# Joining the half-array stays of inverse step 1 in a Fourier-mixing and SoLU kernel

## The chip, the cores and the metric

The kernel runs on one core of a Trainium2 chip. The engines are PE (TensorE, the matmul array), DVE (VectorE), ACT (ScalarE), POOL (GpSimd) and SP (SyncE, whose queue issues all DMAs here). The metric is device time in microseconds of one execution; lower is better. Most runs of one kernel agree within 0.3%.

## What is computed

The input x has 8 batches of 3136 rows and 256 columns, in float32. Each batch goes through a real Fourier transform along its rows, a complex 256 by 256 matrix with a bias, a soft threshold, and the inverse transform. The 25088 rows that result go through an expert layer with a SoLU in the middle.

```python
X = np.fft.rfft(x, axis=1)
Yr = Xr @ w_r - Xi @ w_i + b_r
Yi = Xr @ w_i + Xi @ w_r + b_i
Yr = np.sign(Yr) * np.maximum(np.abs(Yr) - lam, 0.0)
Yi = np.sign(Yi) * np.maximum(np.abs(Yi) - lam, 0.0)
y = np.fft.irfft(Yr + 1j * Yi, n=3136, axis=1)
...
h = y @ w_in
solu = h * softmax(h)
ln = (solu - mean(solu)) / np.sqrt(var(solu) + 1e-06) * g_ln
out = ln @ w_out
```

## The kernel before

**Factors of the transform.** 3136 is 98 times 32. Forward step 1 (`fwd1`, and `fwd1_plain` for batches 0 and 1) multiplies by a 98 by 98 matrix, forward step 2 (`fwd2`) does the 32 with its twiddle factors, and the inverse does the same backwards: inverse step 1 (`inv1`) and inverse step 2 (`inv2`). Between forward step 1 and step 2 a batch goes through DRAM (`s1`), and again between inverse steps 1 and 2 (`s2`). Most operands are split into a high and a low half in fp16, so that a product takes three fp16 matmuls; batch 0, and parts of batch 1, use plain float32 operands.

**Units.** The frequencies of a batch are handled in 13 units (`NU`). Units 0 to 11 have 128 rows of Y: two groups of 64, each with its own matrix. Unit 12 has only 64. For a unit, `fwd2` makes X in PSUM and splits it into `Xh` and `Xl`. `mix` multiplies by the weights (18 matmuls of 256 columns from batch 1 on, into two PSUM banks), adds the scaled bias `bias_y` with the first of two DVE operations that write `yt`, clips into `yc`, takes the difference `y` on POOL, casts it to `yh` on ACT and writes the rest `yl` on POOL.

**Inverse step 1.** For each unit, `inv1` runs for the pairs (yh, high matrix), (yl, high matrix) and (yh, low matrix), with real and imaginary parts each, one matmul for each group of 64 rows. The two matmuls of 64 rows stand on the two halves of the array and run side by side; a run of such matmuls is called a stay on half arrays here. Each of the two groups has its own PSUM bank, 256 columns for each unit. Batch 0 calls `inv1` for one unit at a time. Batches 1 to 7 call it for two units, so that two banks fill, and a stay has 24 matmuls. Behind it ACT copies each bank to the high part of `zout` and DVE writes the low part; then one DMA stores `zout` (512 KB from batch 1 on) to DRAM. The pool has two `zout` buffers.

**The expert layer.** A tile of 128 rows goes through `moe_head` (12 matmuls of 512 columns into two `ph` banks, a maximum `nm` on DVE for each, an Exp on ACT and a product on DVE for each half, into `u`), `moe_turn` (cast to `lh` and difference `ll`, each turned by a transposing DMA to `th` and `tl`) and `moe_tail` (24 matmuls of 256 columns into a `po` bank, one scaled copy, the store). A batch has 24.5 tiles; every second batch gets the shared tile.

**PSUM.** Eight banks are shared by kinds, each with a most: pf=5 (the transform from batch 1 on, inverse step 2 too), ph=5, po=2, and pb=8 for batch 0.

**Order of the work.** Nothing is issued as it is written. Each operation is noted with a key (`nc.key`), and `Plan.order` runs a list scheduler with a model of each engine's times: an engine takes, of the operations that can start within 50 ns of the first, the one with the lowest key. An operation can start when what it needs is done and its tiles have a free buffer and, in PSUM, a free bank. Matmuls in `nc.together()` are one operation for the plan, and `nc.reserve` makes it wait for its output's buffers as well. The order that comes out is fixed in each engine's queue; on the chip, semaphores keep it right.

**Keys of a batch.** `first` is the key of the first head of batch b, L its 24 or 25 tiles. In that time lie `front_b(b + 1)`, that is `fwd2`, `mix` and `inv1` of the next batch, and `front_a(b + 2)`, that is the peaks, the scales and `fwd1` of the one after. In `front_b`, step n does `fwd2` of unit n, `mix` of unit n − 1, and `inv1` of the units up to n − lag.

**Lines that the change touches.** `fa_s` (line 485) is the plain matrix of forward step 1, loaded first of all and used by `fwd1_plain` only (line 633). `Xs` (line 686) is the float32 sum of X's parts, from batch 1 on, with one buffer. `bias_y` is made in `set_scales` (lines 566 and 567) with two buffers, and read at lines 731 and 754. `yh` and `yl` (lines 774 and 775) have four buffers each. `inv1` is lines 780 to 824, `front_b` lines 1144 to 1157, and its keys are at line 1185.

Of the kernel before, what the change touches and what calls it, by code (L numbers as in the profile page):

```python
# [12 lines left out]
F32 = mybir.dt.float32  # L13
F32R = mybir.dt.float32r
BF16 = mybir.dt.bfloat16
F16 = mybir.dt.float16
U32 = mybir.dt.uint32
AF = mybir.ActivationFunctionType
ALU = mybir.AluOpType
# [5 lines left out]
S, N1, N2 = 3136, 98, 32  # L25
H = N1 // 2
Q = (H - 1) // 2
# [5 lines left out]
S_SCALE, B_SCALE, Z_SCALE, X_SCALE = 2.0**-7, 2.0**-5, 2.0**-11, 2.0**-11  # L33

LOW = 2.0**11
# [416 lines left out]
def fft_mix_solu_kernel(ctx: ExitStack, tc, x, w_r, w_i, b_r, b_i, w_in, w_out, g_ln, fa, fbf, fsf, iaf, fa16, fb, fs, gb, gs, ia, out):  # L452
    nc = Plan(tc.nc)
    B, _, D = x.shape
    FF = w_in.shape[1]
    P = 128
    ND = D // P
# [10 lines left out]
    fp = Pool(ctx.enter_context(tc.tile_pool(name="fp", bufs=2)), 2)  # L468
# [4 lines left out]
    def front_psum(b):  # L473

        return banks.tile("pf" if b else "pb")
# [3 lines left out]
    def load(shape, src, name, pool=const, dtype=F32, **kw):  # L479
        t = pool.tile(shape, dtype, name=name, **kw)  # L480
        nc.sync.dma_start(t, src)
        return t

    nc.key = -300
    fa_s = load([N1, N1], fa, "fa_s")
    nc.key = 0
    ident = const.tile([P, P], F32, name="ident")
    ones = const.tile([P, P], F32, name="ones")
# [40 lines left out]
    peaks, scales = {}, {}  # L529
# [13 lines left out]
    def set_scales(b):  # L543

        top = sp.tile([P, 1], F32, name="top", bufs=2)
        pk = peaks.pop(b)
        m = pk.shape[0]
        nc.vector.tensor_reduce(top[:m], pk, AX.X, ALU.max)
        pw = front_psum(b)
        nc.tensor.transpose(pw[:1, :m], top[:m], ident[:m, :m])  # L550
        v = sp.tile([1, 2], F32, name="v", bufs=2)
        nc.vector.tensor_reduce(v[:, :1], pw[:1, :m], AX.X, ALU.max)
        nc.vector.tensor_scalar(v[:, 1:], v[:, :1], gain[:1], bias_top[:1], ALU.mult, ALU.add)
        nc.vector.tensor_scalar(v, v, 2.0**-100, None, ALU.max)
        nc.vector.tensor_scalar(v.bitcast(U32), v.bitcast(U32), 0x7F800000, None, ALU.bitwise_and)
        pw = front_psum(b)
        nc.tensor.matmul(pw[:, :2], ones[:1], v, start=True, stop=True)
        un = sp.tile([P, 4], F32, name="un", bufs=4)
        sc = sp.tile([P, 5], F32, name="sc", bufs=4)
        nc.vector.tensor_scalar(un[:, :2], pw[:, :2], 2.0**-14, None, ALU.mult)  # L560
        nc.vector.tensor_scalar(sc[:, :2].bitcast(U32), un[:, :2].bitcast(U32), -1.0, float(254 << 23), ALU.mult, ALU.add)
        nc.vector.tensor_scalar(sc[:, 4:], sc[:, :1], S_SCALE * B_SCALE, None, ALU.mult)
        nc.vector.tensor_scalar(un[:, 3:], un[:, :1], 1.0 / S_SCALE, sc[:, 1:2], ALU.mult, ALU.mult)
        nc.vector.tensor_scalar(sc[:, 2:3], sc[:, 1:2], LAM, None, ALU.mult)
        nc.vector.tensor_scalar(sc[:, 3:4], sc[:, 1:2], -LAM, None, ALU.mult)
        bias_y = fp.tile([P, 2, D], F32, name="bias_y", bufs=2)
        nc.vector.tensor_scalar(bias_y, bias_t, sc[:, 1:2], None, ALU.mult)
        nc.vector.tensor_scalar(un[:, 2:3], un[:, 3:], w_un, None, ALU.mult)
        scales[b] = dict(
            x=sc[:, 0:1], X=sc[:, 4:], lam=(sc[:, 2:3], sc[:, 3:4]), mix=un[:, 2:3], bias=bias_y, y=un[:, 1:2]  # L570
        )
        if b:
            set_h_scale(b)

# [31 lines left out]
    PLAIN, PLAIN_Z = 2, 1  # L606
# [32 lines left out]
    QG = 4  # L639
    raw, bins = {}, {}  # L640
    s2 = {}
    zouts = {}
    Xs, Ys = {}, {}
# [18 lines left out]
    NU = Q // 2 + 1  # L662
# [96 lines left out]
    def mix(b, u):  # L759
        n, _ = unit_size(u)  # L760
        half = 2 * N2
        M = n * half
        t = mix_split(b, u) if b else mix_first(u)
        c = fp.tile([P, 2, D], F32, name="yc", bufs=2)
        up, down = scales[b]["lam"]
        y = fp.tile([P, 2, D], F32, name="y", bufs=2)
        if b == 0:

            nc.scalar.activation(c[:M], t[:M], AF.Relu, bias=down[:M], scale=-1.0)
            nc.scalar.activation(t[:M], t[:M], AF.Relu, bias=down[:M], scale=1.0)  # L770
        else:
            nc.vector.tensor_scalar(c[:M], t[:M], up[:M], down[:M], ALU.min, ALU.max)
        nc.gpsimd.tensor_sub(y[:M], t[:M], c[:M])
        yh = fp.tile([P, 2, D], F16, name="yh", bufs=4)
        yl = fp.tile([P, 2, D], F16, name="yl", bufs=4)
        nc.scalar.copy(yh[:M], y[:M])
        nc.gpsimd.tensor_sub(yl[:M], y[:M], yh[:M])
        Ys[b, u] = yh, yl

    def inv1(b, u0, u1):  # L780


        n, _ = unit_size(u0)
        half = 2 * N2
        K = half * n
        g, gi = divmod(2 * u0, QG)
        part, dtype = ((2, D), F16) if b >= PLAIN_Z else ((D,), F32)
        if n == 1:
            zo, gi = fp.tile([K, 1, *part], dtype, name="zs", bufs=1), 0
        else:  # L790
            if gi == 0:
                zouts[b] = fp.tile([P, QG, *part], dtype, name="zout")
            zo = zouts[b]
        w = u1 - u0
        pz = [front_psum(b) for _ in range(n)]
        nc.reserve(zo[:, gi : gi + n * w])
        with nc.together():
            for u in range(u0, u1):
                yh, yl = Ys.pop((b, u))
                for k, (t, j) in enumerate(((yh, 0), (yl, 0), (yh, 1))):  # L800
                    for ri in range(2):
                        for i in range(n):
                            rows = slice(i * half, (i + 1) * half)
                            gw = gs_s[:, ri, j] if n == 1 else gb_s[g][rows, u % 2, ri, j]
                            nc.tensor.matmul(
                                pz[i][:K, (u - u0) * D : (u - u0 + 1) * D], gw, t[rows, ri], start=k + ri == 0, stop=k + ri == 3
                            )
        m = n * w
        for i in range(n):
            pv = pz[i][:K, : w * D].rearrange("p (u e) -> p u e", u=w)  # L810
            if b < PLAIN_Z:
                zv = zo[:, gi : gi + m].rearrange("p (u i) e -> p u i e", i=n)[:, :, i]
                nc.scalar.activation(zv, pv, AF.Copy, scale=Z_SCALE)
                continue
            zv = zo[:, gi : gi + m].rearrange("p (u i) t e -> p u i t e", i=n)[:, :, i]
            nc.scalar.activation(zv[:, :, 0], pv, AF.Copy, scale=Z_SCALE)
            nc.vector.scalar_tensor_tensor(zv[:, :, 1], zv[:, :, 0], -LOW, pv, ALU.mult, ALU.add)
        if b >= PLAIN_Z:
            zo = zo.rearrange("p q t e -> p q (t e)")
        if n == 1:  # L820
            nc.sync.dma_start(s2[b][4 * Q :].rearrange("c (n m) -> (c n) m", n=N2), zo[:, 0])
        else:
            v = s2[b][: 4 * Q].rearrange("(q c) m -> q (c m)", c=4).rearrange("q (r m) -> r q m", r=P)
            nc.sync.dma_start(v[:, g * QG + gi : g * QG + gi + m], zo[:, gi : gi + m])

# [206 lines left out]
    bias_t = const.tile([P, 2, D], F32, name="bias_t")  # L1034
# [6 lines left out]
    gs_s = load([2 * N2, 2, 2, 2 * N2], gs, "gs_s", dtype=F16)  # L1041
# [5 lines left out]
    fb_s, gb_s = {}, {}  # L1047
# [95 lines left out]

    def front_b(b, key, step):

        lag = 4 if b == 0 else 3
        for n in range(NU + lag):
            nc.key = key + n * step
            for fn, u in ((fwd2, n), (mix, n - 1)):
                if 0 <= u < NU:  # L1150
                    fn(b, u)
            u = n - lag
            if u == NU - 1 or 0 <= u < NU and b == 0:

                inv1(b, u, u + 1)
            elif 0 < u < NU and u % 2:
                inv1(b, u - 1, u + 1)

    nc.key = -140
    set_scales(0)  # L1160
# [16 lines left out]
    first = 0  # L1177
    for b in range(B):
        L = 24 + b % 2
        if b == 0:  # L1180
            front_a(1, -40, 0.5)
        if b + 2 < B:
            front_a(b + 2, first + 6, (L - 6) / 17)
        if b + 1 < B:
            front_b(b + 1, first + (6 if b == 0 else -2), (L - (8 if b == 0 else 4)) / (NU + 3))
        groups = 0
        for n in range(L):
            while groups < N2 // G2 and groups * G2 * N96 <= n * P:
                nc.key = first + n - 3
                inv2(b, groups)  # L1190
                groups += 1
            nc.key = first + n
            heads.append(moe_head((b, n if n < 24 else None)))
            nc.key = first + n + 0.5
            turned.append(moe_turn(*heads.pop(0)))
            nc.key = first + n + 1
            moe_tail(*turned.pop(0))
        first += L
# [25 lines left out]
```

## Time and profile before

| | us |
|---|---|
| median of 3 runs | 1615.39 |
| lowest and highest | 1613.5 and 1616.07 |
| profiled execution | 1616.65 |
| its span, first to last instruction | 1614.9 |
| PE busy in it | 1577.4 |
| DVE busy | 1326.1 |
| ACT busy | 1238.8 |
| POOL busy | 1123.6 |

The profile is of one execution. Every instruction is recorded under the line of a helper (L342), so its groups are told apart by the tiles that they write and read: `pf<-yh,gb` is a matmul of inverse step 1 that reads yh and the matrix gb. Durations of matmuls overlap, because the array is a pipeline: what one of them costs is read from the starts of the neighbours. In a row of a stretch of time stand its length, the busy time of PE, PE's weight loads, DVE, ACT and POOL, each with a count of instructions, then the granted clock of PE, the share of the DMA engines and GB/s. A row of such a stretch for one tile alone has only the engines that work on it. In a row of a tile stand the least, median and greatest duration in ns and the first and last start in us.

### The profile page before, as it was taken

The numbers are of one execution on the slowest core, as the hardware profiler recorded it, in microseconds if no ns is written. First come the engines' busy times: TensorE is split into PE (matmuls) and PEld (weight loads), VectorE is DVE, ScalarE is ACT, GpSimd is POOL, SyncE is SP. The second block draws the span as 40 slices with busy tenths as digits, with TensorE's granted clock in tenths as the row PEclk, the third lists the DMA queues.
The fourth block names the chain that finished last, engine by engine and source line by source line (L and its number), as shares of the span: only waits on it lengthen the run. The fifth ranks groups of instructions, "written<-read, shape, count | busy, mean of one in ns | idle before, by whom it ended". The sixth has DMA issues, their size and how long they took to land.

```text
span 1614.9 us, 38042 instructions
## 1 busy us (share of the span) xinstructions
PE 1577.4 (98%) x13040; PEld 1126.1 (70%) x13040; DVE 1326.1 (82%) x3423; ACT 1238.8 (77%) x2576; POOL 1123.6 (70%) x1889
## 2 busy tenths in 40 slices
PE   5979999999999999999999999999999999999998
PEld 3545877678766777667776687666876677776675
DVE  4779789996799877898789978899688888877775
ACT  4667678886789867898679876798678877778886
POOL 0555776677866777667777687766976677777676
PEclk8989999999999999999999999999999999999999
DMA  8868955996579965899669984699857986677676
GB/s 236 277 228 206 210 145 133 227 240 155 127 185 232 226 151 121 185 243 217 135 130 224 279 169 118 135 246 258 166 112 165 204 172 129 122 146 154 140 129 115
DMA packets 533923, 290.25 MB, mean 180 GB/s; under 512 B 427642, under 2 KB 503964, under 8 KB 533728
## 3 DMA queue, kind: packets, MB, share of 16 engines
q1 hardware_dynamic: 533728, 287.82, 78.5%
q8 instruction: 102, 1.67, 0.4%
q14 instruction: 93, 0.76, 0.2%
HBM read 107.89 MB, written 77.07 MB: 115 GB/s over the span
## 4 chain that ended last, share of the span: by engine, by line
PE 92%; DVE 3%; ACT 2%; DMA 1%; issue 1%; POOL 0%; SPq 0%; DVEq 0%; ACTq 0%; POOLq 0%
PE po L342 31%; PE ph L342 30%; PE pf L342 27%; PE pb L342 4%; DVE u L342 1%; DVE xl L342 1%; DVE nm L342 1%; DMA zt<-s2f 0%; ACT u L342 0%; DMA s2f<-zs 0%; ACT junk L342 0%; DMA bin<-s1f 0%; DMA s1f<-tl 0%; DVE av L342 0%; DMA th<-lh 0%
## 5 line engine op out<-in xcount | busy, mean ns | idle before, releaser
L342 POOL TENSOR_TENSOR ll<-u,lh 128x1024 f16<-128x1024 f32 x196 | 424.4, 2166 | 98.5 <-ACT lh L342 95.4
L342 PE MATMUL po<-wout,th 128*128 128x256 f16 x3136 | 374.5, 273 | 4.1 <-DMA th<-lh 1.9
L342 PEld LDWEIGHTS <-th 128*128 128x128 f16 x3136 | 305.4, 98 | 64.9 <-issue 4.4
L342 ACT ACTIVATE u<-ph,m,hsb 128x512 f32<-128x512 f32 x384 | 295.9, 776 | 52.3 <-DVE m L342 51.7
L342 DVE TENSOR_REDUCE nm<-ph 128x1 f32<-128x512 f32 x392 | 264.5, 685 | 79.7 <-PE ph L342 78.6
L342 DVE SCALAR_TENSOR_TENSOR u<-ph,ch,u 128x512 f32<-128x512 f32 x392 | 281.5, 747 | 23.1 <-ACT u L342 13.7
L342 PE MATMUL ph<-win_hi,ring_hi 128*128 128x512 f16 x768 | 291.9, 380 | 0.2 <-DVE u L342 0.2
L342 PE MATMUL ph<-win_lo,ring_hi 128*128 128x512 f16 x768 | 291.5, 380 | 0.0
L342 PE MATMUL ph<-win_low,ring_lo 128*128 128x512 f16 x768 | 291.3, 379 | 0.0
L342 ACT CAST lh<-u 128x1024 f16<-128x1024 f32 x196 | 205.7, 1049 | 53.1 <-DVE u L342 52.8
L342 PEld LDWEIGHTS <-ring_hi 128*128 128x128 f16 x1536 | 146.8, 98 | 140.5 <-issue 6.5
L342 ACT ACTIVATE junk<-u,total 128x1024 bf16<-128x1024 f32 x196 | 226.1, 1154 | 7.1 <-POOL total L342 6.6
L342 PE MATMUL po<-wout,tl 128*128 128x256 f16 x1568 | 203.4, 273 | 0.8 <-DMA tl<-ll 0.8
L342 PEld LDWEIGHTS <-tl 128*128 128x128 f16 x1568 | 150.7, 98 | 35.0 <-issue 3.4
L342 POOL TENSOR_TENSOR y<-yt,yc 128x512 f32<-128x512 f32 (+1 forms) x104 | 133.1, 1281 | 59.4 <-ACT yt L342 32.7
L342 POOL TENSOR_TENSOR yl<-y,yh 128x512 f16<-128x512 f32 (+1 forms) x104 | 122.3, 1178 | 40.3 <-ACT yh L342 39.3
L342 PE MATMUL pf<-w_hi,Xh 128*128 128x256 f16 (+1 forms) x546 | 149.1, 273 | 0.0
L342 PE MATMUL pf<-w_hi,Xl 128*128 128x256 f16 (+1 forms) x546 | 148.9, 273 | 0.0
L342 PE MATMUL pf<-w_lo,Xh 128*128 128x256 f16 (+1 forms) x546 | 148.8, 273 | 0.0
L342 ACT ACTIVATE o<-po,r 128x256 f32<-128x256 f32 x196 | 93.2, 475 | 59.6 <-PE po L342 30.7
L342 PEld LDWEIGHTS <-ring_lo 128*128 128x128 f16 x768 | 75.1, 98 | 91.1 <-DVE last_lo L342 0.3
L342 PEld LDWEIGHTS <-Xh 128*128 128x128 f16 (+1 forms) x1196 | 113.9, 99 | 24.8 <-issue 1.9
(196 smaller groups left out, 2922.5 us busy)
## 6 DMA issues: line engine op xcount, KB each, us to landing
xt<-in_x_dram SPq DMA_DIRECT2D x108, 392.0 KB
zt<-s SPq DMA_DIRECT2D x56, 392.0 KB
s<-zout SPq DMA_DIRECT2D x42, 512.0 KB
s<-av SPq DMA_DIRECT2D x48, 392.0 KB
bin<-s SPq DMA_DIRECT2D x36, 512.0 KB
out_dram<-o SPq DMA_DIRECT2D x128, 96.0 KB
out_dram<-o SPq DMA_DIRECT2D x136, 64.0 KB
bin<-s1f SPq DMA_DIRECT2D x12, 512.0 KB
```

The source lines that it names most:

```text
L342: getattr(engine, name)(*args, **kw)
```

## The change

Inverse step 1 takes four units at a time in batches 1 to 7: for units 0 to 3, 4 to 7 and 8 to 11 the 48 matmuls stand in one group, over four PSUM banks, and both `zout` buffers are reserved ahead of it. The evictions and the two stores follow. Batch 0 and unit 12 go as before. For the two more buffers (a fifth `yh` and a fifth `yl`), `bias_y` goes from two buffers to one and is now made in `mix` of a batch's unit 0, and the plain matrix `fa_s` is no tile of its own but lies in the first use of `Xs`. The lag of `inv1` in `front_b` goes from 3 to 2 from batch 1 on, the start of the front's keys from `first` − 2 to `first` − 3 (from batch 2 on), and their step from (L − 4) / 16 to (L − 5) / 16.

```diff
-    fa_s = load([N1, N1], fa, "fa_s")
+
+    fa_s = fp.tile([P, ND, 2, 2 * N2], F32, name="Xs", bufs=1).rearrange("p h i c -> p (h i c)")[:N1, :N1]
+    nc.sync.dma_start(fa_s, fa)
...
-        bias_y = fp.tile([P, 2, D], F32, name="bias_y", bufs=2)
-        nc.vector.tensor_scalar(bias_y, bias_t, sc[:, 1:2], None, ALU.mult)
...
+        if u == 0:
+            scales[b]["bias"] = fp.tile([P, 2, D], F32, name="bias_y", bufs=1)
+            nc.vector.tensor_scalar(scales[b]["bias"], bias_t, scales[b]["up"], None, ALU.mult)
         t = mix_split(b, u) if b else mix_first(u)
...
-        yh = fp.tile([P, 2, D], F16, name="yh", bufs=4)
-        yl = fp.tile([P, 2, D], F16, name="yl", bufs=4)
+        yh = fp.tile([P, 2, D], F16, name="yh", bufs=5)
+        yl = fp.tile([P, 2, D], F16, name="yl", bufs=5)
...
-        pz = [front_psum(b) for _ in range(n)]
-        nc.reserve(zo[:, gi : gi + n * w])
+        work = []
+        for u2 in range(u0, u1, 2):
...
+            us = range(u2, min(u2 + 2, u1))
+            work.append((g, gi, zo, us, [front_psum(b) for _ in range(n)]))
+        nc.reserve(*(zo[:, gi : gi + n * len(us)] for _, gi, zo, us, _ in work))
         with nc.together():
-            for u in range(u0, u1):
...
+            for g, _, _, us, pz in work:
+                for u in us:
+                    yh, yl = Ys.pop((b, u))
+                    for k, (t, j) in enumerate(((yh, 0), (yl, 0), (yh, 1))):
+                        for ri in range(2):
+                            for i in range(n):
+                                rows = slice(i * half, (i + 1) * half)
+                                gw = gs_s[:, ri, j] if n == 1 else gb_s[g][rows, u % 2, ri, j]
+                                at = slice((u - us[0]) * D, (u - us[0] + 1) * D)
+                                nc.tensor.matmul(pz[i][:K, at], gw, t[rows, ri], start=k + ri == 0, stop=k + ri == 3)
+        for g, gi, zo, us, pz in work:
...
-        lag = 4 if b == 0 else 3
+        lag = 4 if b == 0 else 2
...
-            elif 0 < u < NU and u % 2:
-                inv1(b, u - 1, u + 1)
+            elif 0 < u < NU and u % 4 == 3:
+                inv1(b, u - 3, u + 1)
...
-            front_b(b + 1, first + (6 if b == 0 else -2), (L - (8 if b == 0 else 4)) / (NU + 3))
+            front_b(b + 1, first + (6 if b == 0 else -3), (L - (8 if b == 0 else 5)) / (NU + 3))
```

More of the change, by code (lines that the diff above doesn't have):

```diff
@@ L565, in set_scales @@
         nc.vector.tensor_scalar(sc[:, 3:4], sc[:, 1:2], -LAM, None, ALU.mult)
-        bias_y = fp.tile([P, 2, D], F32, name="bias_y", bufs=2)
-        nc.vector.tensor_scalar(bias_y, bias_t, sc[:, 1:2], None, ALU.mult)
         nc.vector.tensor_scalar(un[:, 2:3], un[:, 3:], w_un, None, ALU.mult)
-        scales[b] = dict(
-            x=sc[:, 0:1], X=sc[:, 4:], lam=(sc[:, 2:3], sc[:, 3:4]), mix=un[:, 2:3], bias=bias_y, y=un[:, 1:2]
-        )
+        scales[b] = dict(x=sc[:, 0:1], X=sc[:, 4:], lam=(sc[:, 2:3], sc[:, 3:4]), mix=un[:, 2:3], y=un[:, 1:2], up=sc[:, 1:2])
         if b:
@@ L785, in inv1 @@
         K = half * n
-        g, gi = divmod(2 * u0, QG)
         part, dtype = ((2, D), F16) if b >= PLAIN_Z else ((D,), F32)
[L788 to L794, printed above, removed]
-        pz = [front_psum(b) for _ in range(n)]
-        nc.reserve(zo[:, gi : gi + n * w])
-        with nc.together():
-            for u in range(u0, u1):
[L799 to L824, printed above, removed]
+        work = []
+        for u2 in range(u0, u1, 2):
+            g, gi = divmod(2 * u2, QG)
+            if n == 1:
+                zo, gi = fp.tile([K, 1, *part], dtype, name="zs", bufs=1), 0
+            else:
+                if gi == 0:
+                    zouts[b] = fp.tile([P, QG, *part], dtype, name="zout")
+                zo = zouts[b]
+            us = range(u2, min(u2 + 2, u1))
+            work.append((g, gi, zo, us, [front_psum(b) for _ in range(n)]))
@@ new lines, in inv1 @@
+        for g, gi, zo, us, pz in work:
+            w = len(us)
+            m = n * w
+            for i in range(n):
+                pv = pz[i][:K, : w * D].rearrange("p (u e) -> p u e", u=w)
+                if b < PLAIN_Z:
+                    zv = zo[:, gi : gi + m].rearrange("p (u i) e -> p u i e", i=n)[:, :, i]
+                    nc.scalar.activation(zv, pv, AF.Copy, scale=Z_SCALE)
+                    continue
+                zv = zo[:, gi : gi + m].rearrange("p (u i) t e -> p u i t e", i=n)[:, :, i]
+                nc.scalar.activation(zv[:, :, 0], pv, AF.Copy, scale=Z_SCALE)
+                nc.vector.scalar_tensor_tensor(zv[:, :, 1], zv[:, :, 0], -LOW, pv, ALU.mult, ALU.add)
+            if b >= PLAIN_Z:
+                zo = zo.rearrange("p q t e -> p q (t e)")
+            if n == 1:
+                nc.sync.dma_start(s2[b][4 * Q :].rearrange("c (n m) -> (c n) m", n=N2), zo[:, 0])
+            else:
+                v = s2[b][: 4 * Q].rearrange("(q c) m -> q (c m)", c=4).rearrange("q (r m) -> r q m", r=P)
+                nc.sync.dma_start(v[:, g * QG + gi : g * QG + gi + m], zo[:, gi : gi + m])
```

## The prediction

> **What bounds the kernel now.** I read the page's head first, then busy time by stretches, then PE's waits, then single stretches of PE in order of time.
>
> ```profile
> span 1614.9 us, 38042 instructions
> ...
> PE 1577.4 (98%) x13040; PEld 1126.1 (70%) x13040; DVE 1326.1 (82%) x3423; ACT 1238.8 (77%) x2576; POOL 1123.6 (70%) x1889
> ```
>
> ```profile
> 0.00:40.00 40.00, 22.53 (x75) 13.39 (x76) 16.55 (x37) 17.06 (x35) 3.46 (x10) 0.81 0.81 235
> ...
> 80.00:120.00 40.00, 31.05 (x182) 17.61 (x180) 30.45 (x61) 26.43 (x56) 22.41 (x17) 0.88 0.70 230
> ...
> 1000.00:1200.00 200.00, 199.33 (x1739) 144.81 (x1738) 173.21 (x451) 159.12 (x337) 146.11 (x246) 1.00 0.81 184
> ...
> 1600.00:1615.00 15.00, 8.08 (x69) 6.16 (x67) 2.81 (x10) 5.93 (x12) 6.43 (x12) 1.00 0.52 105
> ```
>
> ```profile
> PE pb L342 <- DMA bin<-s1f: 15.0, 1, 15.0
> PE pf L342 <- DMA zt<-s2f: 8.9, 1, 8.9
> PE po L342 <- DMA th<-lh: 1.9, 2, 1.6
> PE pf L342 <- DVE u L342: 1.5, 1, 1.5
> ```
>
> PE (third column of a stretch) is idle 1614.9 − 1577.4 = 37.5 us. Of these 17.5 lie in the first 40 us, 9.0 in 80 to 120, 6.9 in the last 15: 33.4 in all, 4.1 for the rest. The two long waits are loads at the start, which the change doesn't touch. Behind the start the kernel lasts as long as PE has work, at full clock (1.00), so a microsecond taken off PE's stream comes off the span, if the other engines still keep it fed. How near they are to not doing so shows within one batch:
>
> ```profile
> 345.00:465.00 120.00, 120.00 (x1149) 92.68 (x1148) 94.67 (x246) 88.75 (x188) 93.93 (x148) 1.00 0.68 146
> 465.00:513.00 48.00, 46.54 (x310) 29.84 (x308) 45.91 (x105) 41.82 (x81) 31.56 (x57) 1.00 0.98 230
> 513.00:541.00 28.00, 28.00 (x224) 17.92 (x222) 27.44 (x82) 23.29 (x55) 16.53 (x36) 1.00 1.11 269
> ```
>
> The first row is the stretch with forward step 2, mix and inverse step 1 (the front's second half): PE full, DVE (fifth column) 79%. The second is forward step 1, the third the peaks: DVE 96% and 98%. The 1.46 us that PE lost there is the 1.5 us wait above. So PE sets the end, DVE is close behind in 76 of some 195 us of a batch.
>
> **The change part by part.** *Stays on half arrays.* A stay is a run of matmuls of 64 rows, two side by side. Its price, from PE in order of time:
>
> ```profile
> 1000.05 1.04 PE L342 MATMUL po<-wout,tl 128*128 128x256 f16 x8
> 1000.93 0.38 PE L342 MATMUL ph<-win_hi,ring_hi 128*128 128x512 f16 x1
> ...
> 1016.70 1.04 PE L342 MATMUL po<-wout,tl 128*128 128x256 f16 x8
> 1017.66 0.39 PE L342 MATMUL pf<-yh,gb 64*128 64x256 f16 x4
> 1017.89 0.38 PE L342 MATMUL pf<-yl,gb 64*128 64x256 f16 x4
> 1018.11 0.60 PE L342 MATMUL pf<-yh,gb 64*128 64x256 f16 x8
> 1018.55 0.38 PE L342 MATMUL pf<-yl,gb 64*128 64x256 f16 x4
> 1018.77 0.38 PE L342 MATMUL pf<-yh,gb 64*128 64x256 f16 x4
> 1019.08 0.39 PE L342 MATMUL ph<-win_hi,ring_hi 128*128 128x512 f16 x1
> 1019.31 0.38 PE L342 MATMUL ph<-win_lo,ring_hi 128*128 128x512 f16 x1
> 1019.52 0.38 PE L342 MATMUL ph<-win_low,ring_lo 128*128 128x512 f16 x1
> ```
>
> Read starts, since the durations overlap. Going in: eight po matmuls take 1000.93 − 1000.05 = 0.88 us before a full-array neighbour, but 1017.66 − 1016.70 = 0.96 before the stay: 0.08. Coming out: the last four half matmuls last 1019.08 − 1018.77 = 0.31, where four in the middle take 0.22 (1017.89 to 1018.11): 0.09. The first full matmul afterwards takes 0.23 where the next takes 0.21: 0.01 to 0.02. A stay of two units lasts 1.42 (1017.66 to 1019.08); one more unit inside costs 0.66 (the yl group of unit one to that of unit two, 1017.89 to 1018.55). So four units in one stay take 1.42 + 2 × 0.66 = 2.74 against 2 × 1.42 = 2.84, and the way in and the slow first matmul are paid once instead of twice: 0.10 + 0.09 + 0.01 = 0.20 us less for each pair of stays joined.
>
> ```profile
> L342 PE MATMUL pf<-yh,gb x672: 269/269/280, 198.4 to 1416.7; 64*128 64x256 f16 x168
> ```
>
> A two-unit stay has 16 yh matmuls, so 672 are 42 stays, six for each of seven batches; they become 21. Batch 0 and each batch's odd last unit keep theirs. Sum: 21 × 0.20 = **4.2 us less**, all on PE's stream. The changed bank inside a stay has no row; a changed bank without a changed array (po to ph at 1000.93) costs nothing, so I take nothing, and at worst the 0.10 would be lost on each: 2.1 us.
>
> The Trainium skill, "TensorEngine Tiling (Array Packing)", Key Properties, says that a changed tiling mode drains the array; the trace agrees, with 0.08 going in and 0.09 coming out. By the warm constant of "TensorE: Matmul & The Clock Gate", Single matmul latency (398 cycles at 2.4 GHz, 166 ns), an estimate would be two undrained latencies, 0.33 us a stay, 7.0 us in all and 1608.4 us; the measured 0.20 decides.
>
> *Evictions.* Their number stays; they now come four at a time.
>
> ```profile
> L342 ACT ACTIVATE zout<-pf x84: 573/594/625, 199.9 to 1418.6; 128x512 f16<-128x512 f32 x84
> L342 DVE SCALAR_TENSOR_TENSOR zout<-zout,pf x84: 668/680/690, 200.5 to 1419.5; 128x512 f16<-128x512 f16 x84
> L342 SPq DMA_DIRECT2D s<-zout x42: 365/457/1777, 201.8 to 1422.8; - x42
> ```
>
> Four take 4 × 0.68 = 2.7 us of DVE behind the stay instead of 1.4; what queues behind them are the heads' reductions, and PE waits for those only when it has no other bank. Taken as nothing, because the front's stretch leaves DVE 21% free; its price when that cover is gone is the slow rival's. The two stores of one stay leave SP back to back, so a tail's transpose can stand 0.46 us longer: nothing to 21 × 0.46 = 9.7 us. I take nothing, by the nearest row: PE waited for th twice in the whole run. Both zout buffers must be empty ahead of a stay; the last stores are then about 58 us old (1218 us over 21 stays), and 1.05 MB at the 184 GB/s of the stretch 1000 to 1200 takes 5.7.
>
> *Y's buffers.* A stay holds four of five yh and yl, so the second unit behind it can't cast yh on ACT until the stay's first unit is read, 0.66 us into the stay; behind that cast on ACT stand Exps and evictions, and PE waits for their banks. The plan puts the cast behind the stay by its own clock. Nothing, with 0.66 × 21 = 14 us at the far end.
>
> *Scaled bias and plain matrix.*
>
> ```profile
> L342 DVE TENSOR_SCALAR bias_y<-bias_t,sc x8: 475/479/481, 25.2 to 1225.7; 128x512 f32<-128x512 f32 x8
> ...
> L342 PE MATMUL pf<-xt,fa_s x32: 590/592/672, 94.9 to 134.9; 98*98 98x512 f32 x32
> ...
> L342 ACT ACTIVATE Xs<-pf,sc x13: 367/474/519, 152.4 to 271.6; 128x256 f32<-128x256 f32 x12, 128x128 f32<-128x128 f32 x1
> ```
>
> The bias is the same DVE operation, moved from the scales to ahead of the batch's first yt: at worst 7 × 0.48 = 3.4 us late, at best 0.48 off the chain of the first scales. It needs the scales only, which are long done, and PE has heads while it runs: nothing. The plain matrix lies in Xs; Xs's first writer now waits for the last plain matmul, over by 135.6, and it started at 152.4 anyway: nothing. Its load stays SP's first.
>
> *Keys.* The front gets a start one key lower and a shorter step; step 1's last stay comes at key 13.6 of a batch of 24 instead of 16.8. This moves work between the three stretches but takes none away. I price it in the rivals.
>
> Sum: −4.2 us. The profiled execution took 1616.65 us, 1.3 above the median of the runs, so 1612.4 in its terms and 1615.4 − 4.2 = **1611.2 us** in the median's.
>
> **The rivals.** A difference under about 0.2% (3.2 us) can't be told from none here.
>
> *Slower: banks.* A stay of four starts only when four of pf's five banks are free at one moment. The mix just before it holds two until both yt operations are through:
>
> ```profile
> L342 DVE SCALAR_TENSOR_TENSOR yt<-pf,un,bias_y x91: 724/743/753, 165.6 to 1409.5; 128x512 f32<-128x512 f32 x84, 64x512 f32<-64x512 f32 x7
> L342 DVE SCALAR_TENSOR_TENSOR yt<-pf,un,yt x91: 731/744/753, 167.3 to 1412.2; 128x512 f32<-128x512 f32 x84, 64x512 f32<-64x512 f32 x7
> ```
>
> The place is the start of each batch's front, where hardly a head is there to fill in (reductions nm on DVE, a head has two):
>
> ```profile
> 541.00:587.00 46.00, 2.55 (x7) 1.00 0.89 191
> 587.00:660.00 73.00, 15.77 (x30) 1.00 0.56 124
> ```
>
> If PE stands for both yt there, once a batch, it is 7 × 1.49 = 10.4 us: 1615.4 − 4.2 + 10.4 = 1621.6. At 0.20 us a stay the gain is gone, at (4.2 + 3.2) / 21 = 0.35 it is slower by what can be told. Against it: PE stayed full in 345 to 465 and has tails and inverse step 2 there, which take other banks or one of pf. For it: a batch's front comes denser. The Trainium skill, "TensorEngine Tiling (Array Packing)", PSUM Bottleneck, warns of just this: tiling speeds TensorE, not the emptying of PSUM; in the trace so far no wait of PE names such a bank, so the rule has not bitten with two units a stay.
>
> *No change that can be told.* The gain is there, but the new order, which the planner works out afresh everywhere, brings stalls like the 1.5 us above: one of 0.4 us a batch is 7 × 0.4 = 2.8, and 1614.0 us. Here belongs too that the joined stay saves half (2.1 us, 1613.3).
>
> *Faster than forecast.* The front done earlier leaves more heads for the two stretches where DVE is full, which are PE-rich. Then the mid-run idle of 4.1 us goes as well: 1607.1.
>
> **How the numbers follow.** Forecast (1608.5 to 1612.1) 0.43, faster than that 0.13, no change 0.28, slower 0.16. Together: faster 0.56, same 0.28, slower 0.16. The range is 1606.0 to 1621.5: below lies little of the faster case (0.05), above the slow rival with stalls at more than one stay a batch (0.08). The forecast's own range is 1608.5 to 1612.1.
>
> **What would show it.** The after trace should have 21 stays of 48 matmuls, 2.7 us each, the same 0.08 and 0.09 at their ends, and PE busy some 4 us less with 37 us idle. More idle time ahead of yh's first matmul, released by a DVE yt, shows the slow rival; more idle ahead of po or ph in the forward-1 stretch the second; less idle there the third. Were the span 4 us shorter but PE's idle time changed by more than 2, the sum was right by luck. It is wrong at the root if joined stays still show a gap between units.

## The result, and the profile after

| | before | after |
|---|---|---|
| median of 4 runs, us | 1614.90 | 1623.65 |
| lowest to highest | 1613.5 to 1616.07 | 1623.22 to 1624.36 |
| profiled execution | 1616.65 | 1623.22 |

The ratio is 1.0056, with a 95% interval from 1.0044 to 1.0067: the changed kernel is 8.75 us slower. The forecast was 4.2 us faster, and the range of the prediction ended at 1621.5 us.

The head of the page after, its stretches and PE's waits, in the columns of before:

```profile
span 1621.4 us, 38034 instructions
...
PE 1575.3 (97%) x13040; PEld 1127.6 (70%) x13040; DVE 1339.8 (83%) x3423; ACT 1242.0 (77%) x2576; POOL 1133.2 (70%) x1889
```

```profile
0.00:40.00 40.00, 22.88 (x78) 13.61 (x79) 16.55 (x37) 17.38 (x36) 3.48 (x10) 0.81 0.82 240
80.00:120.00 40.00, 30.94 (x180) 17.88 (x179) 31.58 (x64) 25.99 (x55) 22.93 (x16) 0.87 0.72 234
345.00:465.00 120.00, 117.53 (x1121) 90.45 (x1120) 93.78 (x234) 85.02 (x182) 90.06 (x136) 1.00 0.65 150
...
1605.00:1621.00 16.00, 9.84 (x78) 7.03 (x76) 3.21 (x11) 7.35 (x14) 7.04 (x12) 1.00 0.66 103
```

```profile
PE po L342 <- DMA th<-lh: 5.2, 5, 2.2
PE pf L342 <- DVE xl L342: 2.6, 2, 1.4
PE pf L342 <- DVE yt L342: 1.8, 2, 1.5
...
PE ph L342 <- DVE u L342: 1.2, 1, 1.2
PE po L342 <- DVE av L342: 1.1, 1, 1.1
```

PE is busy 2.1 us less, where some 4 was forecast, and idle for 46.1 us instead of 37.5, where 37 was forecast. The idle time at the start and at the end is as before: 17.1 and 9.1 us in the two early stretches, 6.2 at the end. So the idle time between them went from 4.1 to 13.7 us. It is in no one place: there are five waits for a transposed tile (5.2 us, before two with 1.9), two for xl, two for yt, and single ones for u and av. The front's stretch, where PE had been full, lost 2.5 us.

The stays are as forecast. One of them, from PE in order of time:

```profile
394.46 0.39 PE L342 MATMUL pf<-yh,gb 64*128 64x256 f16 x4
394.69 0.38 PE L342 MATMUL pf<-yl,gb 64*128 64x256 f16 x4
394.91 0.60 PE L342 MATMUL pf<-yh,gb 64*128 64x256 f16 x8
395.34 0.38 PE L342 MATMUL pf<-yl,gb 64*128 64x256 f16 x4
395.56 0.60 PE L342 MATMUL pf<-yh,gb 64*128 64x256 f16 x8
396.00 0.38 PE L342 MATMUL pf<-yl,gb 64*128 64x256 f16 x4
396.22 0.60 PE L342 MATMUL pf<-yh,gb 64*128 64x256 f16 x8
396.65 0.38 PE L342 MATMUL pf<-yl,gb 64*128 64x256 f16 x4
396.87 0.38 PE L342 MATMUL pf<-yh,gb 64*128 64x256 f16 x4
397.19 0.61 PE L342 MATMUL po<-wout,tl 128*128 128x256 f16 x4
```

From 394.46 to 397.19 it takes 2.73 us, against 2.74 worked out, and the step from one unit to the next (394.69, 395.34, 396.00, 396.65) is 0.65 or 0.66 throughout, across the change of banks too. In all 21 stays the way in costs the same 0.10 us as before, and none has idle time of PE ahead of it. So no stay waited for its banks.

One of the new stalls step by step: first POOL, then DVE, then PE, each in order of time.

```profile
413.26 2.13 POOL L342 TENSOR_TENSOR ll<-u,lh 128x1024 f16<-128x1024 f32 x1
```

```profile
412.68 0.69 DVE L342 TENSOR_REDUCE nm<-ph 128x1 f32<-128x512 f32 x1
413.28 2.40 DVE L342 TENSOR_SCALAR yc<-yt,sc 128x512 f32<-128x512 f32 x1
415.59 0.26 DVE L342 TENSOR_SCALAR m<-nm,hsb 128x1 f32<-128x1 f32 x1
...
417.03 0.74 DVE L342 SCALAR_TENSOR_TENSOR yt<-pf,un,bias_y 128x512 f32<-128x512 f32 x1
```

```profile
415.93 0.38 PE L342 MATMUL ph<-win_low,ring_lo 128*128 128x512 f16 x1
417.82 0.70 PE L342 MATMUL pf<-ia_s,zt 98*128 98x98 f16 x12 [1.51 <-DVE yt L342]
```

The clip yc takes 0.54 us in the median. Here it began 0.02 us behind ll on POOL and took 2.40 us, 1.86 more. Everything behind it on DVE came late, and after 415.93 PE had no bank for the next inverse step 2 until a yt was done. The Trainium skill, "SBUF — State Buffer", Who interferes with whom, says that VectorE, in its two-port modes or with two SBUF inputs, and GpSimd take one pair of ports as a lock for a whole instruction, and that the second to come waits; the trace agrees: ll is over at 415.39 (413.26 + 2.13), and yc ends at 415.68, just behind it. With the same 3423 instructions DVE is busy 13.7 us longer after the change. Summing what each DVE operation took beyond the median of its kind, where that is over 0.3 us, gives 21 us before and 35 after; this is called stretched time below.

### The profile page after: what moved, and what is told of

Read it like the earlier page. It is cut to its first block, busy times and chain, and to the rows that moved or that the text cites. A ratio compares the mean times of both kernels' runs of the same rounds, so it can differ in the third digit from the quotient of the medians.

```text
span 1621.4 us, 38034 instructions
## 1 busy us (share of the span) xinstructions
PE 1575.3 (97%) x13040; PEld 1127.6 (70%) x13040; DVE 1339.8 (83%) x3423; ACT 1242.0 (77%) x2576; POOL 1133.2 (70%) x1889
## 4 chain that ended last, share of the span: by engine, by line
PE 80%; DVE 8%; ACT 4%; DMA 4%; issue 3%; POOL 1%; SPq 0%; DVEq 0%; ACTq 0%; POOLq 0%
PE po L342 27%; PE ph L342 25%; PE pf L342 24%; PE pb L342 4%; DVE u L342 2%; DMA th<-lh 2%; DVE nm L342 1%; ACT u L342 1%; DVE xl L342 1%; ACT junk L342 1%; ACT lh L342 1%; DVE av L342 1%; POOL ll L342 1%; DMA zt<-s2f 0%; DVE ring_lo L342 0%
```

## The experiments

Each time is a median, and each ratio is against the kernel before on the same chip (its medians were 1615.7, 1616.1, 1616.0 and 1615.7 us in the four groups of runs). A cost in us is the difference of these medians. There are three theories. S: the stay of four has a price of its own. K: the lag and the keys do it. P: the order itself does it; any new order of the same work runs with more waits, and the kernel before has an uncommonly good one. For the runs on the ports that VectorE and GpSimd share there is a fourth, D: VectorE is late because the transposes are, and its stretched operations only show it.

### One part at a time

**x1**, stays of two in the changed kernel:

```diff
-            elif 0 < u < NU and u % 4 == 3:
-                inv1(b, u - 3, u + 1)
+            elif 0 < u < NU and u % 2:
+                inv1(b, u - 1, u + 1)
```

> The changed kernel, but inverse step 1 in stays of two units again (places, lag and keys as changed). Theory S (the stay of four itself costs: four evictions at once, four banks at once): the 8.75 us go, and the 4.2 us of the joined stays come back as a cost: about 1615. Theory K (denser front by lag and keys): the loss stays and the stays' 4.2 us are added: about 1627.5. Theory P (any new order is followed less well by the chip, because VectorE's operations meet GpSimd's at other moments; no part has a price of its own): anywhere from 1612 to 1630, not near the sum of the parts.

1620.13 us, ratio 1.0026 (1.0011 to 1.0040). Neither 1615 nor 1627.5.

**x2**, old keys in the changed kernel:

```diff
-            front_b(b + 1, first + (6 if b == 0 else -3), (L - (8 if b == 0 else 5)) / (NU + 3))
+            front_b(b + 1, first + (6 if b == 0 else -2), (L - (8 if b == 0 else 4)) / (NU + 3))
```

> The changed kernel with the front's old keys (first - 2, step (L - 4) / 16); stays of four, lag 2 and places as changed. Theory S: the loss stays, 1621 to 1625. Theory K: it goes, 1611 to 1613. Theory P: anywhere from 1608 to 1630.

1624.97 us, 1.0063 (1.0048 to 1.0078). The loss stays.

**x3**, in the kernel before only the places: `yh` and `yl` with five buffers, `bias_y` with one and made in `mix`, `fa_s` in `Xs`, as in the change's diff.

> The kernel before with the places alone: five yh and yl, one scaled bias made in mix, the plain matrix in Xs; stays of two, lag 3, old keys. Theories S and K: 1615, as before. Theory P: anywhere from 1612 to 1630, though PE's work and all stays are those of before.

1618.37 us, 1.0020 (1.0010 to 1.0030).

**x4**, in the kernel before only lag and keys:

```diff
-        lag = 4 if b == 0 else 3
+        lag = 4 if b == 0 else 2
...
-            front_b(b + 1, first + (6 if b == 0 else -2), (L - (8 if b == 0 else 4)) / (NU + 3))
+            front_b(b + 1, first + (6 if b == 0 else -3), (L - (8 if b == 0 else 5)) / (NU + 3))
```

> The kernel before with lag 2 and the new keys alone; stays of two, old places. Theory S: 1615. Theory K: 1615 + 8.75 + 4.2, about 1628. Theory P: anywhere from 1612 to 1630.

1625.66 us, 1.0065 (1.0048 to 1.0082).

The parts don't add. Lag and keys alone cost 10.0 us; with the places as well (x1) the cost is 4.5, though the places alone cost 2.7 (x3). Taking the new keys back doesn't help (x2). K falls as a price of its own: x4 is near its 1628, but x1 should then have taken 1627.5 and x2 1611 to 1613. No run has the old lag beside stays of four, so the lag alone is not tested there. S doesn't hold in its plain form, since with stays of two the kernel is still 4.5 us slower.

### The same work in another order

The planner's patience is the 50 ns within which an operation with a lower key goes first. Another value draws the order anew and leaves the work as it is:

```diff
-    PATIENCE = 50.0
+    PATIENCE = 80.0
```

**x7**, the kernel before at 80 ns:

> The kernel before with nothing changed but the planner's patience (80 ns in place of 50), so the same work in another order. Theory P: anywhere from 1612 to 1630, as far off as the change was; theories S and K and D: 1614 to 1619, since no stay, buffer, key or lag is touched.

**x8**, the changed kernel at 40:

> The changed kernel with nothing changed but the planner's patience (40 ns). Theory P: anywhere from 1610 to 1630; theories S and K: 1621 to 1626, as the changed kernel.

**x10**, the kernel before at 40:

> The kernel before with the planner's patience at 40 ns. Theory P: an order like any other, 1618 to 1632, so that the kernel before is the lucky one of its kind. Theory S: 1614 to 1619.

**x11**, the changed kernel at 80:

> The changed kernel with patience 80. Theory P: 1614 to 1630, and 3 to 6 us less than the kernel before at 80 on average over such pairs (40, 50, 80), since the joined stays save 4.2 in every order. Theory S: more than the kernel before at the same patience.

**x12**, the changed kernel at 100:

> The changed kernel with patience 100, an order that the planner itself puts lowest of some twenty. Theory P: 1610 to 1622, as good as or better than the kernel before. Theory S: 1620 to 1628.

**x13**, **x14** and **x15**, the kernel before at 100 and at 60, the changed kernel at 60:

> The kernel before with patience 100. Theory P (the order drawn decides, the joined stays save some 4 us on average): 1615 to 1632, more than the changed kernel at the same patience (1615.1) by 0 to 10. Theory S: below it.

> The kernel before with patience 60. Theory P: 1616 to 1632, above the kernel before at 50. Theory S: 1614 to 1619.

> The changed kernel with patience 60. Theory P: 1612 to 1630, and over the five pairs (40, 50, 60, 80, 100) a mean difference of -1 to -6 us against the kernel before. Theory S: a mean difference above 0.

| patience | kernel before, us (ratio) | changed kernel, us (ratio) | difference of ratios |
|---|---|---|---|
| 40 | 1620.81 (1.0037) | 1616.93 (1.0008) | −0.29% |
| 50 | 1614.90 (1) | 1623.65 (1.0056) | +0.56% |
| 60 | 1626.55 (1.0068) | 1623.84 (1.0048) | −0.20% |
| 80 | 1631.20 (1.0111) | 1629.78 (1.0089) | −0.22% |
| 100 | 1621.21 (1.0032) | 1615.07 (0.9997) | −0.35% |

The intervals of single ratios are 0.1% to 0.25% to either side. The kernel before in other orders is 0.3% to 1.1% slower, by the medians 5 to 15 us, with not one operation changed; its own order is the best of the five. The changed kernel runs over the same width, 1615 to 1630, and is the faster of the two in four pairs of five; at 40 and 100 that is clear of the intervals, at 60 and 80 it isn't. The mean of the five differences is −0.10%, −1.6 us, and their scatter of 0.37% leaves 0.17% of error on that mean: 2.7 us. So the mean agrees with the 4.2 us that the joined stays save, and can't be told from none. The expectation of 3 to 6 us over the pairs 40, 50 and 80 (x11) failed: their mean is +0.02%. Nor is the changed kernel at 100 a blind draw, since the planner's own model put it lowest of some twenty (x12). What is shown is that the pair at 50 is the odd one, and that orders differ by more than the change is worth.

The pages of these ten runs, one profiled execution each, tell the two sides apart:

| patience | PE busy before, us | PE busy changed, us | PE idle before, us | PE idle changed, us |
|---|---|---|---|---|
| 40 | 1581.1 | 1576.4 | 38.5 | 41.1 |
| 50 | 1577.4 | 1575.3 | 37.5 | 46.1 |
| 60 | 1582.1 | 1576.6 | 41.2 | 41.3 |
| 80 | 1581.5 | 1578.6 | 47.7 | 47.3 |
| 100 | 1579.8 | 1575.7 | 39.0 | 35.6 |

PE is busy less in all five pairs, in the mean by 3.9 us with an error of 0.6, which agrees with the 4.2 of the sum. Its idle time is 1.5 us longer in the mean, with an error of 2.0. So the saving on PE's stream is there in every order, and a small price of the stays of four in idle time (what is left of S) is neither shown nor excluded.

### The price of a stay, with the order held

**x9**: all five queues in the same order as in the changed kernel, with one full-array matmul of two columns in the middle of each of the 21 stays:

```diff
             for g, _, _, us, pz in work:
+                if us[0] > u0:
+                    nc.tensor.matmul(pz[0][:, :2], w_hi[0][:, 0, :P], w_hi[0][:, 0, :2], start=True, stop=True)
                 for u in us:
```

> The changed kernel, every queue in the very same order, with one matmul of 128 rows and two columns between units 1 and 2 of each of the 21 stays, so that the array goes to full and back there; its result is overwritten. The price of a way out and in by the trace is 0.20 us, the matmul itself some 0.05: if PE's stream is on the path all the time, 21 x 0.25 = 5 us more than the changed kernel, 1628 to 1629.5. If stalls elsewhere swallow what PE wins or loses, 1623 to 1625.

1629.30 us, 1.0081 (1.0064 to 1.0098). By the ratios that is 0.25% or 4.0 us over the changed kernel, with an interval of some 0.2% to either side; the bare medians are 5.65 us apart; 5 was expected. PE in order of time, at the middle of such a stay:

```profile
397.21 0.38 PE L342 MATMUL pf<-yh,gb 64*128 64x256 f16 x4
397.53 0.18 PE L342 MATMUL pf<-w_hi 128*128 128x2 f16 x1
397.64 0.39 PE L342 MATMUL pf<-yh,gb 64*128 64x256 f16 x4
```

The last four half matmuls now last 0.32 (397.21 to 397.53) and the small one 0.11, where four had taken 0.22: 0.21 us more. In the two profiles each of the 21 stays shows this, 4.3 us in all. The spans are 6.3 us apart (1621.4 and 1627.7): waits elsewhere came out up to 1.3 us longer or shorter, and the granted clock was 0.54 and 0.50 in two stretches of 3 us (from 421.0 and 1619.5), where it was 1.00 at these places of the changed kernel. So the array's changes cost their full price on PE's stream, as the sum has it; the times agree, but would show it only just.

### The shared port

**x5** and **x6**: each GpSimd operation waits for the last VectorE operation on the shared ports that the plan puts ahead of it. The order in each queue stays.

```diff
+        after = mybir.DependencyInfo(mybir.DependencyClass.Sync, mybir.DependencyReason.DATA)
+        held = None
...
+                if op.port and op.engine == "gpsimd" and held is not None:
+                    tc.add_manual_dep(done.ins, held.ins.name, after, reason="port")
+                if op.port and op.engine == "vector":
+                    held = done
```

> The changed kernel with one more kind of wait: each GpSimd operation waits for the last VectorE operation on two SBUF inputs or in the fast scalar form that the plan puts ahead of it, as the plan's own model has it. Engine work and order in each queue are as changed. Theory P (VectorE's operations stand still behind GpSimd's long ones because GpSimd got there first): stretched VectorE time falls from 35 us to under 10, the loss goes, 1611 to 1617. If the stretched operations are a symptom of lateness that comes from elsewhere (theory D, the transposes and their DMA): 1622 to 1630, since the waits only add.

> The kernel before with the same waits. It has 21 us of stretched VectorE time. Theory P: 1609 to 1615. Theory D: 1615 to 1620.

x5, the changed kernel, took 1621.76 us, 1.0043 (1.0028 to 1.0058); x6, the kernel before, 1615.63, 1.0003 (0.9993 to 1.0013). In x5's rows of tiles, page and waits:

```profile
L344 DVE SCALAR_TENSOR_TENSOR xl<-xt,sc,xh x48: 1264/1277/1287, 251.8 to 1278.9; 98x1024 f16<-98x1024 f32 x48
```

```profile
PE 1577.2 (97%) x13040; PEld 1128.5 (70%) x13040; DVE 1323.3 (82%) x3423; ACT 1241.3 (77%) x2576; POOL 1090.2 (67%) x1889
```

```profile
PE po L344 <- DMA th<-lh: 7.9, 6, 2.4
```

No xl is stretched any more (1287 ns at most, 3182 in the changed kernel), and DVE is busy 16.5 us less. The stretched time fell from 35 to 15 us and not under 10 as expected, since single clips yc still take up to 2153 ns. By the ratios (1.0056 and 1.0043) only some 2 us came back, and the two intervals overlap: PE's waits for xl and yt all but went, and its wait for transposed tiles rose from 5.2 to 7.9 us. The 1611 to 1617 of theory P was wrong for x5, and x6 lies where D had it. So the stretched operations are not the whole cause; and patience 60 on the kernel before is 11 us slower with only 17 us of stretched time.

### A version below both

**x16**: the changed kernel with patience 100 (x12) and the port's waits (x5).

> The changed kernel with patience 100 and GpSimd's waits for VectorE's shared-port operations, as in the run with these waits alone. If they spare 2 us here as there: 1612 to 1614, below both kernels.

1613.48 us, 0.9986 (0.9976 to 0.9996). Its page:

```profile
PE 1578.5 (98%) x13040; PEld 1127.6 (70%) x13040; DVE 1321.8 (82%) x3423; ACT 1239.7 (77%) x2576; POOL 1098.3 (68%) x1889
```

In a span of 1612.2 us PE is idle for 33.7 us, 12.4 less than in the changed kernel. It is below the changed kernel by ten, and below the kernel before by two, which the interval just shows. Its order is the picked one of x12, which alone came to 0.9997, and the port's waits show no gain over that beyond the intervals. So it is the order that took the loss away.

## Why the prediction was wrong

- *The sum for the stays, −4.2 us*: right. A stay takes 2.73 us against 2.74, PE is busy 3.9 us less in the mean of five orders, and x9 pays the price back stay by stay with every queue in the same order.
- *A changed bank inside a stay costs nothing*: right, 0.65 to 0.66 us for every unit.
- *Evictions, Y's buffers, the bias, the plain matrix, each at nothing*: in the changed kernel's profile not one of them shows as a wait of its own. In other orders of it PE does wait for a copy into zout, 1.1 us in x8 (below), 0.8 in x12 and 1.3 in x16, which has x12's order, and with stays of two 0.8 in x4: small, but not nothing everywhere. And x3 has the places of Y, the bias and the plain matrix alone and is 2.7 us slower; none of these places shows as a wait of its own there either, so the order is the likely reason.

```profile
PE pf L342 <- DVE zout L342: 1.1, 2, 0.6
```

- *The slow rival, stays that wait for banks*: right in its sign, wrong in its place. No stay waited; the idle time stands ahead of tails, forward step 1 and inverse step 2. Only the 1.51 us above is a wait for a bank that a yt held, and it is inverse step 2 that waits.
- *The step that failed* is in the rival of no change: "the new order, which the planner works out afresh everywhere, brings stalls like the 1.5 us above: one of 0.4 us a batch is 7 × 0.4 = 2.8". The mechanism was named, but its size was wrong, and so was its place among the rivals, while the sum itself had nothing for it. In the profile the idle time in mid-run rose by 9.6 us (4.1 to 13.7). The size came from the kernel before, as if its 4.1 us of mid-run idle belonged to the work; they belong to its order. The same work in four other orders takes 5 to 15 us more, and its profiles have 9 to 15 us of idle time between start and end. So the redrawing should have been the widest term of the sum, with a sign: four new orders of four were worse than the one at hand.
- *The keys, "takes none away"*: true of the work. But the keys are what the order is drawn by, and x4 is 10 us slower, which lies within the 5 to 15 us that patience alone does.

It stays open what makes one order better than another. The late transposes (1.9 us of PE's waits before, 5.2 after, 7.9 in x5) and the shared ports are two places where an order loses. Neither measures it: x14 is 11 us slower than the kernel before with 2.3 us of waits for th and less stretched time, and x9, in the changed kernel's order, has 3.8 us for th where that kernel has 5.2. No run took the transposes' lateness away.

## What to carry to other kernels

Where a planner draws the order of every queue from a model, a change is two changes: the work, which a trace prices to a tenth of a microsecond, and a new draw of the order, whose width must be measured first, by drawing the old kernel's order anew with nothing else changed. The order at hand may be a good draw, as it was here (the best of five), and an edit gives it up for a new one. To judge the edit, hold the order (as x9 does), compare over several draws, or compare PE's busy time apart from its idle time.

## What the runs showed of the hardware

The array's change between half and full costs the same in all stays of the kernel before, the changed kernel and x9, 0.08 to 0.10 us each way, whichever full-array matmul stands beside it. A VectorE operation that came 0.02 us behind a GpSimd one on the shared ports took 2.40 us instead of 0.54; waits that brought such stretched time from 35 to 15 us gained no more than the intervals leave open. The planner's patience alone moved one core's time by up to 1.1%.
